# Weight conversion three steps earlier and weight splits on a three-step rhythm, in a fused attention and two-layer feed-forward kernel

## The chip, the cores and the metric

The kernel runs on one core of a Trainium2 chip. The metric is the device time of one launch in microseconds. The kernel before takes 812.19 us, the median of three runs (811.95 to 813.73). PE is TensorE's matrix multiply and PEld its weight load, DVE is VectorE, ACT is ScalarE, POOL is GpSimd, and SP is the engine that issues most of the DMAs.

## The reference

```
q_pool = q.reshape(B, H, S // 2, 2, D).mean(axis=3)        # B 4, H 8, S 1152, D 64
scores = (1 / sqrt(D)) * q_pool @ k.T
attn   = softmax(scores)                                    # with 1e-9 in the denominator
x      = (attn @ v) -> heads side by side: (4, 576, 512)
xn     = (x - mean) / sqrt(var + 1e-6) * g_ln
out    = x + relu(xn @ w_ch1) @ w_ch2                       # w_ch1 512x2048, w_ch2 2048x512
```

All inputs and the output are float32.

## The kernel before, in words

**Attention.** The heads are taken in 16 pairs, four pairs for each of the four batches. A pair has nine tiles of 128 query rows against 1152 keys, so there are 16 x 9 = 144 steps, and `step(i)` (L985) writes the instructions of step i. In a step DVE reads the scores out of PSUM and finds the row maxima (`emit_max`, L410), ACT takes the exponential (L417), PE makes the scores of the next step (`emit_s`, L390 and L398) and the product with v of an earlier one (`emit_pv`).

The first 36 steps, which are batch 0, transpose the probabilities on PE (`on_pe`, L364). The steps from 36 on split each probability into a high and a low half in 16 bits. ACT makes the high half (L428). The low half is made by DVE (L437), or, in every third step (`low_on_pool`: i % 9 in 2, 5, 8), by POOL with L239 and L435. It is written one step later, in `emit_lo(i - 1)`, which also issues the transposing DMA on SP (L440). Every product with v is made two steps after its scores in batch 0 and four steps after them from then on.

**Feed-forward layer.** It is cut into units, 24 products of 256 columns (L631) or 12 or 8 products of 512 columns (L663). From step 38 on each step takes one unit from a queue (`some_units`, L962), and after the last step the rest of the queue runs alone on PE. A unit may start only when `w_done` counts enough split blocks of its part of the weights. Units with first number 0 to 3 need part 0 to 3. A unit that isn't ready leaves its step without one. The result of a second-layer unit is added to x on DVE (L677), that of a first-layer unit is written by ACT (L644) and DVE (L645).

**Weights.** The two matrices come as 32 pieces of 512 KB. `w_load(m)` issues the DMA of piece m on SP (L734), in step m. `w_bias(m)` runs on ACT (L739), in step m + 3. `w_conv(m)` puts three instructions on DVE (all seen as L105, the line of `later`) in step m + 4. Eight pieces make one of four parts, 0 to 3. When the last piece of a part is converted, `w_reduce` (L765 to L773, on DVE) and `all_max` find a scale, and `w_scales` calls `w_splits`. Seven buffers hold pieces that wait (`w_place`). Each part has four blocks, and `w_split_a`, `w_split_b` and `w_split_c` split a block into two 16-bit halves on POOL (L239 twice, then L806).

**The order of the work** is written by hand in tables. `at(i, ...)` puts a call at the end of step i, `pre(i, ...)` at its start. The splits of parts 0 and 1 go to the deque `calm`, one per step up to step 34 and two per step from 35 on. Up to step 34 each has a `gate` ahead of it (L241): a small memset on DVE (L244) that a copy on POOL (L245) waits for, so that POOL's next instructions start when DVE has come to that place. The splits of parts 2 and 3 are put in steps 40 to 58, `a`, `b` and `c` of a block in three steps that follow each other, with no gate. Each engine runs its instructions in the order in which they were written, and so does each DMA queue.

**Other names.** `warm(n)` (L1071) runs n products of the identity with itself on PE, whose result isn't used: 84 of them run while the first inputs are loaded. `load` and `load_q` fetch k, v and q of a pair. `bound` (L182, on ACT) finds the largest absolute value of an input. `take_v` (L247) brings v of the next pair into 16-bit halves on POOL, `dup_q` (L166) and `pool_q` (L162) prepare q. The buffers for k and v hold one pair each, so k of pair p + 1 is loaded when the transposes of pair p have been read.

## Time and profile before

| | before |
|---|---|
| median of 3 runs | 812.19 us |
| profiled execution, its own time | 812.42 us |
| its span in the trace | 810.6 us |
| busy: PE, PEld, DVE, ACT, POOL | 96%, 68%, 74%, 67%, 43% of the span |
| the chain that ended last, by engine | PE 65%, DVE 18%, ACT 6%, issue 4%, DMA 3%, POOL 2%, SP's queue 2% |
| step 0 to step 35 (batch 0), by the starts of L410 | 13.65 to 173.28 us |
| step 36 to step 143 | 173.28 to 689 us |
| PE alone with the rest of the units | 689 to 810.6 us |

The profiled execution is 0.23 us above the median of the runs. Its span begins with the first instruction on the core, and 1.8 us of the device time lie around it. A time "at 226.59" is counted from the span's start. A row of the timeline gives the start, the duration, the engine, the line, what is written from what, and in brackets the idle time of that engine just before, with what ended it.

### The profile page before, as it was taken

The page shows a single profiled execution, that of the slowest core. Times are in us where ns is not written, and L with a number is a line of the kernel's source. Part 1 is how long each engine was busy: PE and PEld are TensorE (multiplying, and loading weights), DVE is VectorE, ACT ScalarE, POOL GpSimd, SP SyncE. Part 2 cuts the span into 40 slices and gives each one's busy share as a digit, 9 for nine tenths or more (in the row PEclk, how much of TensorE's full clock was granted, in tenths as well). Part 3 has the DMA queues.
Part 4 walks back from the last instruction along what each step waited for, and adds up shares of the span by engine and source line. Part 5 has one row for each costly group of instructions (what it writes and reads, how often), then busy time and mean ns, then how long its engine had stood idle before and what let it go on. Part 6 is the DMA issues. An engine that isn't in the chain of part 4 may idle for free.

```text
span 810.6 us, 21296 instructions
## 1 busy us (share of the span) xinstructions
PE 782.1 (96%) x8948; PEld 552.8 (68%) x8948; DVE 596.5 (74%) x1175; ACT 545.5 (67%) x789; POOL 346.2 (43%) x338
## 2 busy tenths in 40 slices
PE   8999999989999999989999999999999999999997
PEld 6788888767565656657666666767575757766764
DVE  4699999998898787898777778888786867521121
ACT  4898989876777778787777787777687676211010
POOL 2010243489999953565442535527161533200000
PEclk9999999999999999999999999999999999999999
DMA  8736556216899989897979898987989686401001
GB/s 225 190 121 235 172 155 191 62 63 118 150 177 155 198 148 212 160 211 127 212 135 219 143 215 140 195 159 145 210 131 194 131 147 120 85 1 27 14 1 27
DMA packets 276017, 115.95 MB, mean 143 GB/s; under 512 B 259280, under 2 KB 259280, under 8 KB 275920
## 3 DMA queue, kind: packets, MB, share of 16 engines
q1 hardware_dynamic: 275440, 113.63, 68.6%
q8 instruction: 70, 1.15, 0.6%
q10 hardware_dynamic: 480, 0.95, 0.4%
q14 instruction: 27, 0.22, 0.1%
HBM read 46.14 MB, written 4.72 MB: 63 GB/s over the span
## 4 chain that ended last, share of the span: by engine, by line
PE 65%; DVE 18%; ACT 6%; issue 4%; DMA 3%; POOL 2%; SPq 2%; ACTq 0%; DVEq 0%; POOLq 0%
PE psum L663 19%; PE psum L631 18%; PE psum L390 7%; PE psum L480 7%; PE psum L471 5%; DVE pe L410 5%; DVE hl L437 3%; PE psum L447 3%; DMA vr<-in_v_dram 2%; PE psum L398 2%; ACT pe L417 1%; PE psum L321 1%; SPq L440 1%; DVE kt L271 1%; DVE ht L645 1%
## 5 line engine op out<-in xcount | busy, mean ns | idle before, releaser
L410 DVE CUSTOM_DVE_ANT_0 pe<-psum,nought,sc 128x1152 f32<-128x1152 f32 x144 | 203.1, 1410 | 29.7 <-PE psum L197 12.8
L417 ACT ACTIVATE pe<-pe,nb 128x1152 f32<-128x1152 f32 x144 | 180.3, 1252 | 32.4 <-DVE nb L410 30.9
L663 PE MATMUL psum<-wsl,ht 128*128 128x512 f16 x864 | 196.6, 379 | 2.7 <-DVE ht L645 2.1
L631 PEld LDWEIGHTS <-wsl 128*128 128x128 f16 x1920 | 169.6, 98 | 26.1 <-issue 8.5
L631 PE MATMUL psum<-xn,wsl 128*128 128x256 f16 x1536 | 176.3, 273 | 7.5 <-DVE xb L677 3.8
L663 PEld LDWEIGHTS <-ht 128*128 128x128 f16 x864 | 81.2, 98 | 91.0 <-issue 3.1
L428 ACT ACTIVATE hl<-pe 128x1152 f16<-128x1152 f32 x108 | 125.6, 1163 | 3.4
L390 PE MATMUL psum<-kt,qt 64*128 64x512 f16 (+1 forms) x960 | 119.7, 380 | 0.9 <-ACT qt L274 0.7
L644 ACT ACTIVATE ht<-psum 128x512 f16<-128x512 f32 x72 | 42.7, 593 | 113.7 <-PE psum L631 111.0
L437 DVE SCALAR_TENSOR_TENSOR hl<-pe,hl 128x1152 f16<-128x1152 f32 x72 | 113.3, 1573 | 0.0
L480 PE MATMUL psum<-vt,pt 128*128 128x65 f16 (+2 forms) x3240 | 106.8, 193 | 0.0
L645 DVE SCALAR_TENSOR_TENSOR ht<-psum,ht 128x512 f16<-128x512 f32 x72 | 49.3, 685 | 69.8 <-ACT ht L644 69.7
L480 PEld LDWEIGHTS <-pt 128*128 128x128 f16 (+1 forms) x3240 | 98.4, 100 | 2.6 <-issue 0.2
L239 POOL TENSOR_SCALAR pe<-pe 128x1152 f32<-128x1152 f32 x36 | 41.5, 1152 | 114.4 <-ACT hl L428 114.4
L435 POOL TENSOR_TENSOR hl<-pe,hl 128x1152 f16<-128x1152 f32 x36 | 85.6, 2378 | 3.0
L471 PE MATMUL psum<-pt,vt 128*65 128x128 f32 (+1 forms) x720 | 77.4, 263 | 1.2 <-DVE kt L271 1.2
L471 PEld LDWEIGHTS psum<-pt,vt 128*65 128x65 f32 x720 | 71.4, 138 | 1.6 <-DVE kt L271 1.4
L390 PEld LDWEIGHTS <-qt 64*128 64x128 f16 (+1 forms) x960 | 31.5, 96 | 47.2 <-issue 28.8
L398 PEld LDWEIGHTS <-qt 128*128 128x128 f16 (+1 forms) x320 | 17.6, 99 | 64.2 <-issue 64.0
L245 POOL COPY gate<-gate 128x1 f32<-128x1 f32 x27 | 5.0, 186 | 106.7 <-DVE gate L244 106.7
L677 DVE SCALAR_TENSOR_TENSOR xb<-psum,inv,xb 128x512 f32<-128x512 f32 x32 | 23.8, 744 | 36.3 <-PE psum L663 36.1
L453 ACT COPY pt<-psum 128x512 f32<-128x512 f32 x72 | 44.5, 637 | 8.1 <-PE psum L447 6.9
(116 smaller groups left out, 968.4 us busy)
## 6 DMA issues: line engine op xcount, KB each, us to landing
stage<-in_moe_w_ch_dram SPq DMA_DIRECT2D x32, 512.0 KB, 7.1
kr<-in_k_dram SPq DMA_DIRECT2D x16, 576.0 KB, 4.8
vr<-in_v_dram SPq DMA_DIRECT2D x16, 576.0 KB, 4.9
qr<-in_q_dram SPq DMA_DIRECT2D x31, 288.0 KB, 4.9
out_dram<-xb SPq DMA_DIRECT2D x28, 128.0 KB, 3.3
pt<-hl SPq DMA_TRANSPOSE x108, 5.6
kr<-in_k_dram SPq DMA_DIRECT2D x16, 64.0 KB, 4.2
out_dram<-xb ACTq DMA_DIRECT2D x4, 128.0 KB, 2.6
```

Of the source, the lines that this page charges most:

```text
L390: nc.tensor.matmul(out=sp[o:o + w, c0:c0 + 512], lhsT=qt[r:r + 64, qa, q0:q0 + w], rhs=kt[r:r + 64, ka, h], start=(a == 0), stop=(a == 2),)
L410: nc.vector.tensor_tensor_reduce(out=st["pe"], in0=st["s"], in1=nought[:, 0:1].to_broadcast([128, S]), scale=pair[i // C]["sc"][:, 0:1], s ...
L417: nc.scalar.activation(out=st["pe"], in_=st["pe"], func=ACTF.Exp, scale=-1.0, bias=st["nb"])
L428: nc.scalar.activation(out=hl[:, 0], in_=st["pe"], func=ACTF.Copy, scale=2.0 ** 15)
L435: nc.gpsimd.tensor_tensor(hl[:, 1], st["pe"], hl[:, 0], op=ALU.subtract)
L437: nc.vector.scalar_tensor_tensor(hl[:, 1], st["pe"], 2.0 ** 15, hl[:, 0], op0=ALU.mult, op1=ALU.subtract)
L453: nc.scalar.copy(st["pt"][:, a:b], st["s"][:, a:b])
L471: nc.tensor.matmul(out=ps[0:65, q0:q0 + w], lhsT=vt[:, h, c], rhs=pt[:, 128 * u + q0:128 * u + q0 + w], start=(u == 0), stop=(u == C - 1),)
L480: nc.tensor.matmul(out=dst[:, 0:n], lhsT=pt[:, a + u, q0:q0 + w], rhs=vt[:, h, c, x0:x0 + n], start=(u == 0 and a == 0 and n == 65), stop= ...
L631: nc.tensor.matmul(out=ps[:, o:o + n], lhsT=wsl[:, 8 * w + cc, wa, f * 128:f * 128 + 128], rhs=xn[:, xa * KD + cc, 0:n], start=(m == 0), s ...
L645: lambda: nc.vector.scalar_tensor_tensor(lo, pv, 0.0, hi, op0=ALU.max, op1=ALU.subtract),
L663: nc.tensor.matmul(out=ps, lhsT=hv[0][:, ha, f, t * 128:t * 128 + 128], rhs=wsl[:, 8 * w + 4 + f // 2, wa, (f % 2) * DM:(f % 2) * DM + DM] ...
```

## The change

Four things are changed.

- Pieces 0, 1 and 2 of the weights are loaded ahead of the steps, pieces 0 and 1 even before v of pair 0 and q of pair 1. From then on piece m is loaded in step m - 3, biased in step m (pieces 0 and 1 ahead of or in step 0, piece 2 in step 0) and converted in step m + 1. `w_reduce` moves three steps with it, and so do the splits of parts 0 and 1.
- `warm(84)` becomes `warm(72)`.
- The splits of parts 2 and 3 (eight blocks, three calls each) are put in steps 40 to 62, one block every third step: a gate with `a` and `b` in one step, a gate with `c` in the next, and no split in the third.
- In those steps the first `take_v` of a pair moves one step later (42, 51 and 60 in place of 41, 50 and 59).

```diff
+    SPLITS = 40
...
         for n in range(2):
+            u = i0 + (5, 7)[n]
             if on_pe(p * C):
-                at(i0 + (5, 7)[n], gate)
-            at(i0 + (5, 7)[n], take_v, p, n)
+                at(u, gate)
+            elif n == 0 and SPLITS <= u < SPLITS + 24:
+                u += 1
+            at(u, take_v, p, n)
...
     for m in range(32):
-        i0 = m
-        pre(i0, w_load, m)
-        at(i0 + 3, w_bias, m)
-        pre(i0 + 4, w_conv, m)
+        if m > 2:
+            pre(m - 3, w_load, m)
+        if m > 1:
+            at(m if m > 2 else 0, w_bias, m)
+        pre(m + 1, w_conv, m)
         if m % 8 == 7:
-            at(i0 + (5 if m < 16 else 4), w_reduce, m // 8)
+            at(m + (2 if m < 16 else 1), w_reduce, m // 8)
...
-            i0 = 22 + 9 * part + 5 * n // 2
-            for x, fn in ((0, w_split_a), (1, w_split_b), (2, w_split_c)):
-                at(i0 + x, fn, 4 * part + n)
+            i0 = SPLITS + 12 * (part - 2) + 3 * n
+            at(i0, gate)
+            at(i0, w_split_a, 4 * part + n)
+            at(i0, w_split_b, 4 * part + n)
+            at(i0 + 1, gate)
+            at(i0 + 1, w_split_c, 4 * part + n)
...
         load(0, "k", nc.sync)
+        w_load(0)
+        w_load(1)
+        load(0, "v", nc.sync)
         load_q(1, (nc.sync,))
-        load(0, "v", nc.sync)
+        w_load(2)
...
-        warm(84)
+        warm(72)
...
         k8_lo()
+        w_bias(0)
         emit_s(0)
         waiting.clear()
         until(q_parts[1], 7)
+        until([lambda: w_bias(1)])
         waiting.add(7)
```

**SP, the DMA queue, at the start.** `kr`, `qr` and `vr` are k, q and v, `stage` is a piece of the weights, `gsb` the gain of the layer norm. The first rows are those before, from q of pair 1 to the pieces behind v of pair 1. The second are the changed ones, behind k of pair 0.

```order
L129 DMA qr<-in_q_dram 64x1152 x2
L121 DMA vr<-in_v_dram 128x2x576
L1084 DMA gsb<-in_moe_g_ln_dram 128x4x1
L734 DMA stage<-in_moe_w_ch_dram 128x1024
L117 DMA kr<-in_k_dram 128x2x576
L118 DMA kr<-in_k_dram 128x2x64
L121 DMA vr<-in_v_dram 128x2x576
L734 DMA stage<-in_moe_w_ch_dram 128x1024 x5
```

```order
L734 DMA stage<-in_moe_w_ch_dram 128x1024 x2
L121 DMA vr<-in_v_dram 128x2x576
L129 DMA qr<-in_q_dram 64x1152 x2
L734 DMA stage<-in_moe_w_ch_dram 128x1024
L1098 DMA gsb<-in_moe_g_ln_dram 128x4x1
L734 DMA stage<-in_moe_w_ch_dram 128x1024
L117 DMA kr<-in_k_dram 128x2x576
L118 DMA kr<-in_k_dram 128x2x64
L121 DMA vr<-in_v_dram 128x2x576
L734 DMA stage<-in_moe_w_ch_dram 128x1024 x5
```

Before, one piece stood ahead of k of pair 1, and now four do.

**POOL in steps 42 to 45.** `wsl` is a block of weights that is split, `vt<-vr` and `vr<-vr` belong to `take_v`, `pe<-pe` and `hl<-pe,hl` are the low half that POOL makes. Before, from the end of step 42 to the split behind the low half in step 45:

```order
L806 TENSOR_TENSOR wsl<-wsl 128x1024
L239 TENSOR_SCALAR wsl<-wsl,gs_83 128x1024
L239 TENSOR_SCALAR vt<-vr,s 128x9x64
L239 TENSOR_SCALAR vr<-vr,s 128x576
L266 TENSOR_TENSOR vt<-vr,vt 128x9x64
L239 TENSOR_SCALAR wsl<-wsl 128x1024
L166 COPY qr<-qr 128x9x64
L806 TENSOR_TENSOR wsl<-wsl 128x1024
L239 TENSOR_SCALAR pe<-pe 128x1152
L435 TENSOR_TENSOR hl<-pe,hl 128x1152
L239 TENSOR_SCALAR wsl<-wsl,gs_83 128x1024
```

Now, from `take_v` in step 43 to the low half in step 45:

```order
L239 TENSOR_SCALAR vt<-vr,s 128x9x64
L239 TENSOR_SCALAR vr<-vr,s 128x576
L266 TENSOR_TENSOR vt<-vr,vt 128x9x64
L245 COPY gate<-gate 128x1
L239 TENSOR_SCALAR wsl<-wsl,gs_83 128x1024
L239 TENSOR_SCALAR wsl<-wsl 128x1024
L166 COPY qr<-qr 128x9x64
L245 COPY gate<-gate 128x1
L807 TENSOR_TENSOR wsl<-wsl 128x1024
L239 TENSOR_SCALAR pe<-pe 128x1152
L435 TENSOR_TENSOR hl<-pe,hl 128x1152
```

The splits stand behind gates, and none follows the low half.

**DVE in step 62**, from one row maximum (the `ISA` at L410) to the next. Before:

```order
L410 ISA pe,nb<-psum,nought,sc 128x1152
L410 ISA nb 128x1
L677 SCALAR_TENSOR_TENSOR xb<-psum,inv_90,xb 128x512
L271 SCALAR_TENSOR_TENSOR kt<-psum,s,kt 128x512
L437 SCALAR_TENSOR_TENSOR hl<-pe,hl 128x1152
```

Now, with the gates at the ends of steps 61 and 62:

```order
L244 MEMSET gate 128x1
L410 ISA pe,nb<-psum,nought,sc 128x1152
L410 ISA nb 128x1
L528 TENSOR_SCALAR r<-psum,s 128x1
L529 RECIPROCAL r<-r 128x1
L271 SCALAR_TENSOR_TENSOR kt<-psum,s,kt 128x512
L437 SCALAR_TENSOR_TENSOR hl<-pe,hl 128x1152
L244 MEMSET gate 128x1
```

The result of a second-layer unit (L677) is gone from step 62. The units that stood in steps 61 and 62 need the last block of part 3, which is now split in steps 61 and 62. They are taken from step 63 on, and every later unit moves with them: by two steps up to step 74, which had none before, and by one step from there to the end.

## Rows read from the trace of the kernel before

**Rows 1.** The page's part 1: busy time, share of the span, instructions.

```profile
PE 782.1 (96%) x8948; PEld 552.8 (68%) x8948; DVE 596.5 (74%) x1175; ACT 545.5 (67%) x789; POOL 346.2 (43%) x338
```

**Rows 2.** PE's waits, 191.03 to 232.14 us: engine, line, releaser, total, times, longest.

```profile
PE psum L631 <- DVE xb L677: 1.6, 1, 1.6
PE psum L631 <- DVE ht L645: 1.1, 2, 0.8
```

**Rows 3.** PE's waits, 232.14 to 292.7 us.

```profile
PE psum L631 <- DVE xb L677: 1.4, 1, 1.4
PE psum L631 <- DVE ht L645: 1.4, 2, 0.7
```

**Rows 4.** PE's waits, 314.36 to 357.08 us.

```profile
PE psum L631 <- DVE ht L645: 0.3, 1, 0.3
```

**Rows 5.** Timeline of steps 45 to 47.

```profile
218.18 1.40 DVE L410 CUSTOM_DVE_ANT_0 pe<-psum,nought,sc 128x1152 f32<-128x1152 f32 x1
...
219.74 2.13 POOL L806 TENSOR_TENSOR wsl<-wsl 128x1024 f16<-128x1024 f32 x1
...
221.84 1.15 POOL L239 TENSOR_SCALAR pe<-pe 128x1152 f32<-128x1152 f32 x1
...
223.07 2.38 POOL L435 TENSOR_TENSOR hl<-pe,hl 128x1152 f16<-128x1152 f32 x1
...
223.43 3.24 DVE L437 SCALAR_TENSOR_TENSOR hl<-pe,hl 128x1152 f16<-128x1152 f32 x1
...
226.59 1.40 DVE L410 CUSTOM_DVE_ANT_0 pe<-psum,nought,sc 128x1152 f32<-128x1152 f32 x1
...
229.03 1.14 PE L631 MATMUL psum<-xn,wsl 128*128 128x256 f16 x9 [1.65 <-DVE xb L677]
```

**Rows 6.** Groups on DVE, 314.36 to 357.08 us: count, busy us, mean ns, idle before.

```profile
L437 DVE SCALAR_TENSOR_TENSOR hl<-pe,hl 128x1152 f16<-128x1152 f32 x7 | 9.5, 1360 | 0.0
```

**Rows 7.** Stretches: length, busy of PE, PEld, DVE, ACT, POOL (instructions), clock, DMA share, GB/s.

```profile
7.20:9.00 1.80, 1.80 (x33) 1.80 (x32) 0.91 (x2) 1.17 (x4) 0.38 (x2) 1.00 1.00 218
9.00:13.65 4.65, 3.53 (x34) 2.38 (x33) 2.50 (x8) 1.89 (x4) 1.43 (x4) 1.00 0.88 254
```

**Rows 8.** Timeline of the start, 9 to 22 us.

```profile
9.49 0.27 PE L197 MATMUL psum<-ident,acc 128*2 128x128 f32 x1
...
14.13 0.37 SPq L117 DMA_DIRECT2D kr<-in_k_dram  x1
...
21.31 1.15 ACT L182 ACTIVATE kt<-kr 128x1152 f16<-128x1152 f32 x1
...
21.44 0.35 DVE L271 SCALAR_TENSOR_TENSOR qt<-psum,s,qt 128x128 f16<-128x128 f32 x1 [1.58 <-ACT qt L274]
```

**Rows 9.** DVE's conversions (L105) alone, steps 3 to 31: length, busy (instructions), clock, DMA.

```profile
24.83:150.76 125.93, 47.98 (x84) 1.00 0.56 170
```

**Rows 10.** Timeline of steps 33 to 35.

```profile
162.04 1.42 DVE L410 CUSTOM_DVE_ANT_0 pe<-psum,nought,sc 128x1152 f32<-128x1152 f32 x1
...
162.41 0.18 POOL L245 COPY gate<-gate 128x1 f32<-128x1 f32 x1
...
169.89 0.66 PE L321 MATMUL psum<-ident,qr 128*128 128x128 f32 x4 [1.16 <-DVE xn L593]
...
172.41 0.55 DVE L765 TENSOR_SCALAR wtop<-wtop 128x8 f32<-128x8 f32 x1
...
173.20 0.16 DVE L773 TENSOR_REDUCE wmax<-wtop 128x1 f32<-128x8 f32 x1
```

**Rows 11.** Timeline of steps 61 and 62: the two units on PE.

```profile
297.06 2.75 PE L663 MATMUL psum<-wsl,ht 128*128 128x512 f16 x12
...
302.13 1.90 PE L663 MATMUL psum<-wsl,ht 128*128 128x512 f16 x8
```

**Rows 12.** Steps 61 to 63, and steps 74 and 75, with the columns of rows 7.

```profile
292.75:306.00 13.25, 13.25 (x174) 7.41 (x173) 10.42 (x19) 10.07 (x15) 7.76 (x7) 1.00 0.96 186
352.30:361.80 9.50, 8.50 (x116) 5.97 (x116) 8.89 (x16) 7.97 (x12) 4.76 (x4) 1.00 1.06 212
```

## The prediction

> **What bounds the kernel now.** The page's busy shares come first: PE is busy for 96% of the span [rows 1], so 28.5 us of the span are PE's idle time, and a change that leaves PE's work as it is can win no more than a part of these. The question is where PE waits, and for whom. I asked for PE's waits stage by stage. From step 40 to step 47 its two largest groups are 1.6 us for L677 and 1.1 us for L645 on DVE [rows 2], and from there to step 60 they are 1.4 and 1.4 us [rows 3]. In the stretch of batch 2 without splits, 42.7 us long, only 0.3 us for L645 is left, and none for L677 [rows 4]. So DVE is late in steps 40 to 60, in the steps in which POOL splits weights.
>
> Why it is late is to be seen in steps 45 to 47 [rows 5]. DVE's low half (L437) begins at 223.43 and takes 3.24 us, where its mean is 1.36 us in the stretch without splits [rows 6]. POOL's own low half (L435) runs from 223.07 to 225.45, and L437 ends 1.2 us after that, so it waited for L435 and then ran at its usual pace. The row maximum of step 47 follows at once (226.59), and PE waits 1.65 us at 229.03 for the L677 behind it. POOL itself came to its low half late, since a split (L806, 2.13 us) stood ahead of it.
>
> **The change, part by part.** The sum is made against the profiled execution, 812.42 us, which is 0.23 us above the median of 812.19. About 0.2% (1.6 us) is what a measurement of this kernel can tell from no change.
>
> *Twelve idle products less.* The last ones ran at 33 in 1.80 us, 55 ns each [rows 7], so twelve are 0.65 us. The transposes and the product L197 that begins the first scale (at 9.49 [rows 8]) stand behind them on PE, and everything to step 0 behind that. I take -0.6. If k arrives too late to begin sooner it is -0.3.
>
> *Loads ahead.* On SP, pieces 1, 2 and 3, 1.57 MB, are now ahead of k of pair 1. At the 254 GB/s of the start [rows 7] that is 6.2 us more in the queue. Before, k was issued at 14.13 and ACT read it at 21.31 [rows 8], 7.2 us later, of which its own 0.66 MB take 2.6. So 4.6 us of the 6.2 are covered, and the queue can be moving pieces before 14.13 as well. I take +0.4, with 0 and +1.2 as the ends. ACT stands in front of L182 for that, with its copies out of PSUM and the exponential of step 2 behind it. V of pair 0 and q of pair 1 come later by up to two pieces, but POOL, which takes them, has nothing else to do there.
>
> *Conversion in steps 1 to 3.* A conversion is three DVE instructions, 47.98 us for 84, so 1.71 us [rows 9]. In step 1 DVE is idle for 1.58 us before L271 [rows 8], waiting for ACT. The 0.1 us that is over falls under ACT's work there. The bias of pieces 0 to 2 lies in ACT's gaps ahead of step 1. I take 0, at most +0.5, which the loads' upper end holds. In steps 4 to 31 each step has the same work as before, with another piece.
>
> *Steps 32 to 35.* The last three conversions leave steps 33 to 35, and `w_reduce` of part 3 moves from step 35 to step 32. It takes 0.9 us, from 172.41 to 173.36 [rows 10], and in step 32 DVE works without a pause up to the row maximum, so the exponential and PE's transposes of step 33 come 0.9 us later. In step 34 1.71 us of conversion go, and PE's wait of 1.16 us at 169.89 for L593 on DVE [rows 10] goes with them. Net -0.3. The ends are -1.2, if the reduction is hidden, and +0.9, if the wait stays.
>
> *Splits on POOL, steps 35 to 60.* POOL has four splits fewer left from batch 0, and those of parts 2 and 3 start behind a gate. The gate's copy began 0.37 us after the row maximum that followed it (162.41 against 162.04) and took 0.18 [rows 10], so `a` and `b`, or `c`, run beside L410, which takes 1.40 us beside POOL's work too (226.59 [rows 5]). What is behind the waiting gate on POOL is the low half of the next step. In step 45 it would end at 0.55 + 2.13 + 1.15 + 2.38 = 6.2 us after the row maximum, against 7.3 before (218.18 to 225.45), L437 1.2 us after that, and the row maximum of step 47 7.4 us after 218.18 in place of 8.4. That cuts 0.9 from the wait of 1.65. The wait of 1.4 us in rows 3 has the same place in the next pair of heads, so I take 1.7 for both. Of the 2.5 us for L645 [rows 2, 3] 0.7 stay, by the 0.3 in 42.7 us of rows 4, and of the other 1.8 I take two thirds, 1.2. Together -2.9. The ends are -4.8, if all but the 0.7 goes, and 0.
>
> That arithmetic lets L437 wait until POOL's instruction has ended. The Trainium skill says so as a rule: in "SBUF — State Buffer", section "Who interferes with whom", a VectorE instruction with two inputs in SBUF contends with a GpSimd instruction that reads SBUF, and the loser is blocked until the other ends. The 1.2 us after the end of L435 agree. If the two shared the port instead, L437 would be stretched by less at step 47, the 1.65 us would nearly go, and the term would be -4.2 in place of -2.9.
>
> *Two steps without a unit.* Steps 61 and 62 lose theirs, 2.75 and 1.90 us of PE [rows 11], as part 3 is done only in step 62. In steps 61 to 63 PE has no idle time in 13.25 us, DVE is busy for 10.42 and ACT for 10.07 [rows 12]. So these steps can shrink by 2.8 us at most, and 1.8 of the 4.65 is lost there. The work comes back later: step 74 had no unit, with PE idle for 1.0 us around it [rows 12], and the other unit adds its whole time at the end, where PE works alone. At best the sum is +0.8. I take +1.2, since three steps seldom run at DVE's bound, and if they don't shrink at all it is 4.65 - 1.0 = +3.65.
>
> *The sum:* -0.6 + 0.4 - 0.3 - 2.9 + 1.2 = -2.2, so 810.2 us. The gates' memsets on DVE, 16 of them, are beside the row maximum and cost nothing that I can see.
>
> **The rivals.**
>
> *All the waits go (806.6 us).* POOL has no backlog any more and DVE none to wait for: -0.6 - 1.2 - 4.8 + 0.8 and the loads hidden, -5.8. For it speaks that the stretch without splits shows next to no such waits. Against it, that the low half on POOL stays, with 2.38 us in L435.
>
> *The waits move (812.0 us).* DVE is earlier, but PE then waits for ACT or for the next bank, and only 0.7 of the 2.9 is won: -0.6 + 0.4 - 0.3 - 0.7 + 1.2 = 0. That is 812.4, and with half of the next 0.8 us won 812.0. PE's share of 96% speaks for it [rows 1]: a wait that is shortened leaves little before the next one. Against it, that rows 4 show a stretch of the same work with hardly a wait.
>
> *Held splits make POOL's low half late (815.8 us).* POOL works in order, and `c` waits for DVE while the low half stands behind it. From the step in which POOL has no backlog, the hold and `c` put the low half 0.55 + 2.13 = 2.7 us behind, with its transposing DMA, the load of the next v behind that on SP, and ACT, which waits for v. Before, steps 57 to 63 had few splits. If the 2.7 us reach ACT once, at the v loaded in step 63, and the waits of DVE stay: -0.6 + 0.4 - 0.3 + 0 + 1.2 + 2.7 = +3.4. Against it, in step 45 the low half comes earlier, by the arithmetic above.
>
> **How the numbers follow.** The forecast has 0.48, the first rival 0.12, the second 0.28, the third 0.12. The likeliest case's own range is 808.6 to 811.6. The range is 806.6 to 813.8: it holds the forecast and the second rival with the loads or the units at their upper ends, and reaches to the first. Faster by over 0.2% (under 810.6) are the first rival and 0.42 of the forecast's 0.48, 0.54. Slower (over 813.8) is the third with a little of the second, 0.13. The rest, 0.33, is the same.
>
> **What would show it.** In the changed profile the products before L285 end 0.6 us sooner. L182 on k of pair 1 waits for its DMA by no more than 1 us. L437 in steps 40 to 53 has a mean under 2.0 us, and PE's wait for L677 in step 47 is under 1 us. Steps 61 to 63 take 10.4 to 12 us, and the tail behind the last row maximum is some 2.6 us longer. The forecast is wrong if the waits for L645 and L677 keep their size, if ACT waits for k or v by 2 us or more, or if steps 61 to 63 don't get shorter.

## The result, and the profile after

The changed kernel takes 823.36 us, the median of four runs (821.32 to 824.14), against 812.88 us for the kernel before in the same comparison. The ratio is 1.0126, with a 95% interval of 1.0109 to 1.0142. It is 10.5 us slower. The forecast was 810.2 us, and its range ended at 813.8. The profiled execution took 823.51 us, with a span of 821.7 us.

First the page, its busy shares [rows 1] and the line of its part 4 that gives the chain that ended last, by engine:

```profile
PE 787.8 (96%) x8936; PEld 553.8 (67%) x8936; DVE 587.5 (71%) x1195; ACT 544.1 (66%) x789; POOL 339.4 (41%) x358
...
PE 71%; DVE 11%; POOL 8%; ACT 5%; issue 3%; DMA 1%; SPq 1%; POOLq 0%; DVEq 0%; ACTq 0%
```

PE is busy for 5.7 us longer, for 12 products less, and POOL, which had 2% of the chain before, has 8%. To see where, both executions were cut at the starts of L410. By step 40 the changed kernel is 1.1 us late; it lost 1.23 in step 0. From step 40 to step 66 it needs 5.6 us more than the 123.3 us of before (2.3 in steps 40 to 60, 3.3 in steps 61 to 65), from step 66 to the last row maximum 1.7 more, and for the tail behind that 2.6 more. These add up to the 11 us between the spans.

PE's waits, with the columns of rows 2, in steps 40 to 47 [rows 2], 48 to 60 [rows 3], and 61 to 65:

```profile
PE psum L631 <- DVE xb L677: 2.0, 1, 2.0
PE psum L631 <- DVE ht L645: 0.6, 2, 0.3
...
PE psum L631 <- DVE xb L677: 2.7, 1, 2.7
PE psum L631 <- DVE ht L645: 0.6, 2, 0.3
...
PE psum L663 <- POOL wsl L807: 2.4, 1, 2.4
PE psum L663 <- POOL wsl L239: 0.9, 1, 0.9
```

The waits for L645 have shrunk as forecast. Those for L677 have grown from 1.6 and 1.4 us, and PE waits for a split itself (L807 is `w_split_c`, which was L806 before). DVE's wait for POOL, steps 40 to 65, and the group of L437 in steps 40 to 60, first before, then now:

```profile
DVE pe L410 <- POOL hl L435: 4.5, 2, 2.3
```

```profile
L437 DVE SCALAR_TENSOR_TENSOR hl<-pe,hl 128x1152 f16<-128x1152 f32 x14 | 29.9, 2136 | 0.0
...
L437 DVE SCALAR_TENSOR_TENSOR hl<-pe,hl 128x1152 f16<-128x1152 f32 x14 | 21.5, 1537 | 0.0
```

So DVE's low half waits far less for POOL, 1.54 us in the mean and not 2.14. But the row maximum now waits twice for POOL's low half, which the kernel before shows nowhere in these steps. The timeline of steps 45 to 47 has the first of the two [rows 5]:

```profile
215.94 1.31 POOL L245 COPY gate<-gate 128x1 f32<-128x1 f32 x1
...
217.13 1.41 DVE L410 CUSTOM_DVE_ANT_0 pe<-psum,nought,sc 128x1152 f32<-128x1152 f32 x1
...
217.22 1.12 POOL L239 TENSOR_SCALAR wsl<-wsl,gs 128x1024 f32<-128x1024 f32 x1
...
220.03 0.19 POOL L245 COPY gate<-gate 128x1 f32<-128x1 f32 x1
...
220.17 2.13 POOL L807 TENSOR_TENSOR wsl<-wsl 128x1024 f16<-128x1024 f32 x1
...
222.28 1.16 POOL L239 TENSOR_SCALAR pe<-pe 128x1152 f32<-128x1152 f32 x1
...
222.81 1.84 DVE L437 SCALAR_TENSOR_TENSOR hl<-pe,hl 128x1152 f16<-128x1152 f32 x1
...
223.53 3.35 POOL L435 TENSOR_TENSOR hl<-pe,hl 128x1152 f16<-128x1152 f32 x1
...
226.91 1.42 DVE L410 CUSTOM_DVE_ANT_0 pe<-psum,nought,sc 128x1152 f32<-128x1152 f32 x1 [2.26 <-POOL hl L435]
...
229.37 1.54 PE L631 MATMUL psum<-xn,wsl 128*128 128x256 f16 x9 [2.05 <-DVE xb L677]
```

Read it from the end. PE waits for L677, which stands behind the row maximum of step 47. DVE is free at 224.65, but the row maximum begins at 226.91, when L435 has ended. The tile `pe` has three buffers (L408), so the row maximum of step 47 writes the buffer that the low half of step 44 is still read from. And L435 is late because POOL came to it late, and because L437 had begun 0.7 us before it: it took 3.35 us, against 2.38 before. No gate kept POOL waiting here: neither row of L245 has idle time before it. The last one that did, for 1.29 us, was at 203.28, and from there on POOL had no pause. It came from `take_v` at 215.94, and then `a`, `b`, the copy of q and `c` stood in a row ahead of the low half.

Step 64 has the third wait. The unit there was written behind the splits of the last block, since `w_done` counts a split when it is written, not when POOL has run it:

```profile
309.48 0.38 PE L663 MATMUL psum<-wsl,ht 128*128 128x512 f16 x1 [0.92 <-POOL wsl L239]
...
309.98 0.19 POOL L245 COPY gate<-gate 128x1 f32<-128x1 f32 x1
...
310.13 2.12 POOL L807 TENSOR_TENSOR wsl<-wsl 128x1024 f16<-128x1024 f32 x1
...
312.30 2.29 PE L663 MATMUL psum<-wsl,ht 128*128 128x512 f16 x5 [2.44 <-POOL wsl L807]
```

### The profile page after: what moved, and what is told of

The parts are those of the page before. It is cut to its first block, busy times and chain, and to the rows that moved or that the text cites. A ratio compares the mean times of both kernels' runs of the same rounds, so it can differ in the third digit from the quotient of the medians.

```text
span 821.7 us, 21307 instructions
## 1 busy us (share of the span) xinstructions
PE 787.8 (96%) x8936; PEld 553.8 (67%) x8936; DVE 587.5 (71%) x1195; ACT 544.1 (66%) x789; POOL 339.4 (41%) x358
## 4 chain that ended last, share of the span: by engine, by line
PE 71%; DVE 11%; POOL 8%; ACT 5%; issue 3%; DMA 1%; SPq 1%; POOLq 0%; DVEq 0%; ACTq 0%
PE psum L631 21%; PE psum L663 19%; PE psum L390 8%; PE psum L480 8%; PE psum L471 5%; DVE pe L410 3%; PE psum L447 3%; PE psum L398 3%; POOL hl L435 2%; POOL vt L266 1%; PE psum L321 1%; DVE hl L437 1%; ACT pe L417 1%; POOL wsl L239 1%; POOL wsl L807 1%
## 5 line engine op out<-in xcount | busy, mean ns | idle before, releaser
L410 DVE CUSTOM_DVE_ANT_0 pe<-psum,nought,sc 128x1152 f32<-128x1152 f32 x144 | 203.2, 1411 | 34.1 <-PE psum L197 14.1
L631 PE MATMUL psum<-xn,wsl 128*128 128x256 f16 x1536 | 179.6, 275 | 8.2 <-DVE xb L677 5.2
L437 DVE SCALAR_TENSOR_TENSOR hl<-pe,hl 128x1152 f16<-128x1152 f32 x72 | 104.0, 1444 | 0.0
L645 DVE SCALAR_TENSOR_TENSOR ht<-psum,ht 128x512 f16<-128x512 f32 x72 | 49.3, 685 | 75.4 <-ACT ht L644 75.4
L435 POOL TENSOR_TENSOR hl<-pe,hl 128x1152 f16<-128x1152 f32 x36 | 87.9, 2442 | 3.0
L245 POOL COPY gate<-gate 128x1 f32<-128x1 f32 x47 | 11.0, 234 | 122.8 <-DVE gate L244 122.8
L677 DVE SCALAR_TENSOR_TENSOR xb<-psum,inv,xb 128x512 f32<-128x512 f32 x32 | 23.9, 746 | 45.8 <-PE psum L663 45.6
```

The lines of the kernel that those rows point to most:

```text
L410: nc.vector.tensor_tensor_reduce(out=st["pe"], in0=st["s"], in1=nought[:, 0:1].to_broadcast([128, S]), scale=pair[i // C]["sc"][:, 0:1], s ...
L435: nc.gpsimd.tensor_tensor(hl[:, 1], st["pe"], hl[:, 0], op=ALU.subtract)
L437: nc.vector.scalar_tensor_tensor(hl[:, 1], st["pe"], 2.0 ** 15, hl[:, 0], op0=ALU.mult, op1=ALU.subtract)
L631: nc.tensor.matmul(out=ps[:, o:o + n], lhsT=wsl[:, 8 * w + cc, wa, f * 128:f * 128 + 128], rhs=xn[:, xa * KD + cc, 0:n], start=(m == 0), s ...
L645: lambda: nc.vector.scalar_tensor_tensor(lo, pv, 0.0, hi, op0=ALU.max, op1=ALU.subtract),
```

## The experiments

Theory P: a held split puts POOL's low half off, it keeps the `pe` buffer, and DVE and then PE wait. The rivals: L, the earlier loads and conversions cost; C, the shorter run of idle products disturbs TensorE's clock for the whole program; U, blocks 14 and 15 are done too late, and the units that are missing or moved cost. The granted clock is among the rivals because the changed profile shows four stretches of 3.4 us at about half clock, in step 0 and behind each of the three waits. Steps are counted by the starts of L410, and all ratios are to the kernel before, with 95% intervals. Each experiment is made from the changed kernel unless it says otherwise.

### The parts of the change, one at a time

84 products put back:

```diff
-        warm(72)
+        warm(84)
```

> The changed kernel (823.4 us), with the 84 idle products of before. Theory P (the held splits put off POOL's low half, its pe buffer and the last split, so that TensorE stands in steps 47, 56 and 64, and its clock falls behind each of these waits): only the first of the four half-clock stretches, in step 0, can go; it cost 1.23 us there against 0.56 us gained by the shorter run of products, so 822.2 to 823.4 us, with the waits of 2.05, 2.69 and 2.44 us in steps 47, 56 and 64 still there. Rival C (the shorter run of products at the start leaves the clock in a state in which it falls again later): no half-clock stretch anywhere, 812 to 816 us.

823.91 us, ratio 1.0140 (1.0123 to 1.0156), 0.5 us above P's range. The four half-clock stretches are all there, in the same places. Rival C falls, and so do the forecast's 0.6 us: with 84 products step 0 began at 12.44 us here, with 72 at 13.09.

The early conversion alone (with 84 products, and `take_v` and the splits as before):

```diff
-            i0 = SPLITS + 12 * (part - 2) + 3 * n
-            at(i0, gate)
...
+            i0 = 22 + 9 * part + 5 * n // 2
+            for x, fn in ((0, w_split_a), (1, w_split_b), (2, w_split_c)):
+                at(i0 + x, fn, 4 * part + n)
```

> The kernel before with the weights' loads, bias, conversion and reduction three steps earlier, and nothing else (84 products, the old places of the splits). Theory P: the early conversion does little: by the changed kernel's steps +1.3 us in steps 1 to 9 of which 1.23 is the half-clock stretch, -1.5 in steps 33 to 35; so 811 to 813.5 us (before: 812.9), and no wait of TensorE over 1.7 us in steps 40 to 64. Rival L (the earlier loads and conversions are what costs, through DMA queues and ACT in the first steps, and shift all that follows): 816 to 823 us.

811.40 us, ratio 0.9983 (0.9973 to 0.9993). Rival L falls: this part is a small gain.

The new places of the splits alone, in the kernel before:

```diff
-            i0 = 22 + 9 * part + 5 * n // 2
-            for x, fn in ((0, w_split_a), (1, w_split_b), (2, w_split_c)):
-                at(i0 + x, fn, 4 * part + n)
+            i0 = SPLITS + 12 * (part - 2) + 3 * n
+            at(i0, gate)
...
+                u += 1
```

> The kernel before with the new places of the second batch's splits alone (steps 40 to 62, each held behind VectorE's copy, and the value's first half a step later); loads, conversion and the 84 products as before. Theory P: nearly all of the loss, 821 to 824 us, with TensorE's waits for L677 of 2 us or more in steps 47 and 56, for the split in step 64, three half-clock stretches behind them and a tail 2.6 us longer. Rivals C and L: 812 to 815 us, of which 1.2 us or so for the units missing in steps 61 and 62.

826.25 us, ratio 1.0168 (1.0151 to 1.0185), above P's range. All of the loss is in this part. PE's waits are 2.84, 2.66 and 2.44 us in steps 47, 56 and 64. But the granted clock was full from 5.7 us until PE had finished in this profile, so one step of Theory P falls: the half-clock stretches are not needed for the loss.

72 products alone, in the kernel before:

```diff
-        warm(84)
+        warm(72)
```

> The kernel before with 72 idle products in place of 84, and nothing else. If the shorter run is what lets the clock fall in step 0 (at 14.5 us in the changed kernel): a half-clock stretch there, -0.56 and +1.23 us, so 813.2 to 813.9 us. If it is the earlier bias and conversion of weights, or the wait for k's DMA with them: no half-clock stretch, -0.6 us, 812.0 to 812.6 us. Rival C (the state of the clock carries through the program): several half-clock stretches, 816 us or more.

815.19 us, ratio 1.0029 (1.0017 to 1.0040), with no half-clock stretch in the profile. None of the three expectations fits. The profiled run was the fastest of ten (813.33), so it can't show where the others lost their time. In it, steps 66 to 75 took 1.1 us longer and steps 118 to 121 0.8 us. Why 72 products cost 2 us here, and nothing measurable in the changed kernel, stays open.

### The hold, and what stands behind it

No gates in front of the second batch's splits:

```diff
-            at(i0, gate)
...
-            at(i0 + 1, gate)
```

> The changed kernel without the gates in front of the second batch's splits, all else in its place. Theory P (c, held for VectorE, stands right ahead of POOL's low half, which keeps a pe buffer that the row maximum three steps on must write): c and the low half start up to 0.9 us sooner, TensorE's waits for L677 in steps 47 and 56 go back to the 1.65 and 1.44 us of before or less, and the last split ends some 0.7 us sooner in step 64: 819 to 822.5 us (changed kernel 823.4). Theory U (what costs is that blocks 14 and 15 are done too late: units missing in steps 61 and 62, TensorE waiting for the last split, every later unit in another step): no change by the gates, 822.5 to 824.5 us, with the wait in step 64 at 2 us or more.

818.72 us, ratio 1.0079 (1.0058 to 1.0101), 0.3 us below P's range. The waits in steps 47 and 56 are 1.50 and 0.67 us, and the row maximum never waits for L435. The gates alone cost 0.47% of the time of before, some 4 us. Against the changed kernel the profile is 4.6 us shorter in steps 40 to 60 and some 3 us in steps 61 to 65, where the last splits aren't held either.

The rhythm one step earlier, so that `c` isn't right in front of the low half:

```diff
-    SPLITS = 40
+    SPLITS = 39
```

> The changed kernel with the rhythm begun in step 39 in place of 40: c then stands in steps 40, 43, ... 61, two steps ahead of POOL's low half and not right in front of it, and each block is done one step sooner. Theory P: TensorE's waits for L677 in steps 47 and 56 are under 1.2 us, 818 to 821 us. Theory U: the waits there matter little; one missing unit and one step's delay less, 820.5 to 823 us, with waits in steps 47 and 56 of which nothing is said.

816.43 us, ratio 1.0056 (1.0035 to 1.0076), below both ranges. Steps 47 and 56 are as P expected (no wait over 0.5 us in step 47, 0.83 us in step 56). What is left is the unit that waits for the last split, now in step 63:

```profile
PE psum L663 <- POOL wsl L807: 4.8, 1, 4.8
```

Part 3 alone back in its old places:

```diff
+            if part == 3:
+                for x, fn in ((0, w_split_a), (1, w_split_b), (2, w_split_c)):
+                    at(49 + 5 * n // 2 + x, fn, 4 * part + n)
+                continue
```

> The changed kernel with part 3 alone back in its old places (steps 49 to 58, a, b and c in three steps, no gates); part 2 keeps the new rhythm. Theory U: the loss is part 3's lateness, so it goes nearly whole: tail and step 64 as before, 811 to 813 us. Theory P: the wait in step 47 stays at 2 us or more, the one in step 56 goes back to 1.4, and part 2's share of the waits stays: 813 to 816 us. If neither place matters (the loss comes from the value's first half half a step later): 820 us or more.

822.93 us, ratio 1.0130 (1.0109 to 1.0150): a miss for both theories, and in the range of the third expectation, by which the later `take_v` (the value's first half) is what costs. The tail is as before and no unit waits for a split, so Rival U's part is gone, and the time is the same. Half of its loss is in steps 40 to 65, and there in step 56, where PE waits 5.6 us. There POOL has `a`, the second half of the value, `b`, the copy of q and `c` in a row ahead of its low half, with no gate at all, and the releaser is the same:

```profile
272.27 2.36 POOL L435 TENSOR_TENSOR hl<-pe,hl 128x1152 f16<-128x1152 f32 x1
...
274.67 1.42 DVE L410 CUSTOM_DVE_ANT_0 pe<-psum,nought,sc 128x1152 f32<-128x1152 f32 x1 [3.49 <-POOL hl L435]
```

So the low half on POOL hurts whenever the work ahead of it makes it late, held or not. `take_v` is a part of that work, and no run moves it alone, so its share isn't shown. The other half of this kernel's loss, 5.4 us, lies behind step 66, 3.4 of it in steps 118 to 121, and is not explained.

All low halves of steps 41 to 62 on VectorE:

```diff
-        return i % C in (2, 5, 8)
+        return i % C in (2, 5, 8) and not 40 < i < 63
```

> The changed kernel with VectorE making all low halves of the probabilities in steps 41 to 62, seven or eight of which POOL made. Theory P: nothing stands behind a held split on POOL that the row maximum needs, so TensorE's waits for L677 in steps 47 and 56 are under 1 us; VectorE has 8 x 1.36 = 10.9 us more work in 22 steps, which it has room for (70% busy there): 817 to 821 us. Theory U: 822 to 824.5 us, since block 15 is no sooner. If VectorE has no room: 825 us or more, with waits for L645 in many steps.

813.64 us, ratio 1.0006 (0.9992 to 1.0020), below what any theory expected. With nothing behind the splits that DVE needs, the time is that of before again, though the gates, the missing units and the longer tail are all still there. Steps 40 to 65 take 5.3 us less than before the change and 10.9 less than in the changed kernel: 6.3 in steps 40 to 60, and 4.6 in steps 61 to 65, where POOL also comes to the last splits sooner (PE waits 1.2 us for them, not 3.4). So the edit takes both waits away and doesn't by itself tell Theory P from Rival U. The group of L437 in steps 40 to 60:

```profile
L437 DVE SCALAR_TENSOR_TENSOR hl<-pe,hl 128x1152 f16<-128x1152 f32 x21 | 31.0, 1478 | 0.1
```

21 low halves cost DVE 31.0 us, where 14 took 21.5 in the changed kernel: 9.5 us more. DVE is busy for 88.4 of the 97.7 us there, so it has room for them. (In the kernel before, 14 took 29.9.)

### Is the rhythm good without POOL's low half?

The same edit in the kernel before, and nothing else:

> The kernel before with VectorE making all low halves of the probabilities in steps 41 to 62, and nothing else. Theory P': POOL's low half among the splits is what makes TensorE wait in steps 45 to 60 of the kernel before too (1.65 and 1.44 us for L677, and the waits for L645), and VectorE pays little for seven more low halves, since it then waits less for the port (in the changed kernel with this edit 21 took 31.0 us, where 14 took 29.9 before): 808 to 810 us (before 812.2). Rival R (the edit only repairs what the held splits spoil): 811.5 to 813.5 us.

812.53 us, ratio 0.9997 (0.9987 to 1.0007): Rival R. In steps 40 to 60 the splits, which stand in their old places there, still get in the way of L437:

```profile
L437 DVE SCALAR_TENSOR_TENSOR hl<-pe,hl 128x1152 f16<-128x1152 f32 x21 | 39.3, 1872 | 0.1
```

That is 9.4 us more than the 29.9 of 14 in the kernel before. So the seven more cost DVE about as much here as in the changed kernel, and the expectation's premise, that VectorE pays little, was wrong: it had set two different kernels against each other.

The profile shows steps 40 to 65 2.1 us shorter, but by step 40 this execution had lost 3.0 us, with half-clock stretches at 14.4 and 178.2 us. Why the median of the others shows no gain either is open.

The early conversion and this edit, with the old places of the splits:

> The kernel before with the early conversion alone (84 products, old places of the splits, 1.4 us faster in its own run) and all low halves on VectorE in steps 41 to 62. Theory P': both gains stand beside each other, 806.5 to 809 us. Rival R: 810.5 to 812 us, the gain of the early conversion alone.

809.87 us, ratio 0.9967 (0.9955 to 0.9980), between the two ranges. This is the kernel to hold the 813.64 us above against. With all low halves on VectorE the rest of the change (the new places and the 12 products less) costs 3.8 us, with POOL's it costs 12.0 (823.36 against 811.40). So about a third of the loss stays when POOL makes no low half there. In steps 40 to 60 alone the new places of the splits lose 4.0 us with POOL's low halves (+2.3 against -1.8 us) and win 3.0 without them (-4.0 against -1.1).

The changed kernel with this edit and the rhythm from step 39:

> The changed kernel with all low halves on VectorE in steps 41 to 62 and the rhythm begun in step 39. If units that are missing or moved cost their 2.6 us in the tail and little else (813.6 us with the rhythm from 40): the tail is as before and the last splits are done a step sooner, 809 to 812 us. If TensorE's wait for the last split only moves one step ahead (4.83 us in step 63 of the run from 39 with POOL's low halves): 813 to 816 us.

811.33 us, ratio 0.9978 (0.9965 to 0.9992), in the range of the first expectation: the tail is back to 126.7 us, and the wait for the last split is 1.1 us.

The changed kernel with this edit and no gates:

> The changed kernel with all low halves on VectorE in steps 41 to 62 and no gates in front of the second batch's splits. Theory P (a gate costs by what stands behind it on POOL): with no low half on POOL the hold is nearly free, so taking the gates away wins under 1.5 us, 812 to 814 us, where it won 4.7 us with the low halves on POOL. Rival G (the hold costs by itself, through the splits that end later): 808 to 811 us.

815.86 us, ratio 1.0039 (1.0023 to 1.0056), slower than with the gates (1.0006), against both expectations. So the hold in front of the splits is worth 2 to 3 us as long as nothing that DVE needs stands behind it on POOL, and costs some 4 us if something does. In the profile the gain is in steps 40 to 60, 2.1 us, where L437 has a mean of 1478 ns with the gates and 1657 without. In steps 61 to 65 the gates cost 1.2. The profiled execution was the fastest of five, so it doesn't show the whole difference.

### Which gate

The gate in front of `c` taken away:

```diff
-            at(i0 + 1, gate)
```

> The changed kernel (823.4 us) without the gate in front of c; a and b stay held. Theory P, in its sharper form (the gate on c does it, as POOL's low half stands right behind c): the row maximum no longer waits for L435 in steps 47 and 56, and the gain of taking all gates away (818.7 us) is nearly all here: 817.5 to 820 us. If the gate on a and b does it: 822 us or more.

The gate in front of `a` and `b` taken away:

```diff
-            at(i0, gate)
```

> The changed kernel without the gates in front of a and b; c stays held. Theory P, sharper form: the row maximum still waits for L435 by some 2 us in steps 47 and 56, 821.5 to 824 us. If the gate on a and b does it: 817.5 to 820 us.

Without `c`'s gate 817.72 us, ratio 1.0065 (1.0043 to 1.0088), as P expected. Without the other one 825.08 us, ratio 1.0142 (1.0122 to 1.0163), 1.1 us above its range. Of the two gates it is the one on `c` that costs. Without it steps 40 to 60 are 3.3 us shorter, and steps 61 to 65 3.7, where the last `c` isn't held. DVE's wait in the run without the gate on `a` and `b`, then in that without `c`'s:

```profile
DVE pe L410 <- POOL hl L435: 4.5, 2, 2.3
```

```profile
DVE pe L410 <- POOL hl L435: 2.3, 1, 2.3
```

One of the two waits, in step 47, outlives `c`'s gate, which P did not expect. The rows of steps 45 to 47 above show that no gate kept POOL waiting there: `a`, `b` and `c` stand ahead of that low half, held or not. How the gate works in the other one is to be seen in steps 50 to 56, first of the changed kernel:

```profile
244.01 1.05 POOL L239 TENSOR_SCALAR wsl<-wsl 128x1024 f16<-128x1024 f32 x1
...
248.39 0.18 POOL L245 COPY gate<-gate 128x1 f32<-128x1 f32 x1 [3.33 <-DVE gate L244]
...
248.53 2.13 POOL L807 TENSOR_TENSOR wsl<-wsl 128x1024 f16<-128x1024 f32 x1
...
250.63 1.15 POOL L239 TENSOR_SCALAR pe<-pe 128x1152 f32<-128x1152 f32 x1
...
251.86 2.37 POOL L435 TENSOR_TENSOR hl<-pe,hl 128x1152 f16<-128x1152 f32 x1
...
268.19 1.53 DVE L437 SCALAR_TENSOR_TENSOR hl<-pe,hl 128x1152 f16<-128x1152 f32 x1
...
268.61 3.36 POOL L435 TENSOR_TENSOR hl<-pe,hl 128x1152 f16<-128x1152 f32 x1
...
272.00 1.42 DVE L410 CUSTOM_DVE_ANT_0 pe<-psum,nought,sc 128x1152 f32<-128x1152 f32 x1 [2.26 <-POOL hl L435]
```

Then of the kernel without `c`'s gate:

```profile
241.43 1.05 POOL L239 TENSOR_SCALAR wsl<-wsl 128x1024 f16<-128x1024 f32 x1
...
242.56 2.13 POOL L807 TENSOR_TENSOR wsl<-wsl 128x1024 f16<-128x1024 f32 x1
...
246.62 1.16 POOL L239 TENSOR_SCALAR pe<-pe 128x1152 f32<-128x1152 f32 x1 [1.94 <-ACT hl L428]
...
247.86 2.38 POOL L435 TENSOR_TENSOR hl<-pe,hl 128x1152 f16<-128x1152 f32 x1
...
264.55 2.37 POOL L435 TENSOR_TENSOR hl<-pe,hl 128x1152 f16<-128x1152 f32 x1
...
266.20 1.94 DVE L437 SCALAR_TENSOR_TENSOR hl<-pe,hl 128x1152 f16<-128x1152 f32 x1
...
268.07 1.41 DVE L410 CUSTOM_DVE_ANT_0 pe<-psum,nought,sc 128x1152 f32<-128x1152 f32 x1
```

Held, POOL stands idle for 3.33 us and then does `c` when it should already be at the low half. From `b` to the end of that low half it takes 10.2 us; free, `c` fills the time in which POOL would wait for ACT anyway, and it takes 8.8. In the steps that follow POOL has the two halves of the value and another block to do and doesn't catch up. So the next L435 comes 0.4 us behind L437 and not 1.65 us ahead of it, and ends 2.25 us behind the end of L437, where the row maximum could have started.

One gate, with `a`, `b` and `c` together behind the low half, from step 39:

```diff
-            i0 = SPLITS + 12 * (part - 2) + 3 * n
...
             at(i0, w_split_b, 4 * part + n)
-            at(i0 + 1, gate)
-            at(i0 + 1, w_split_c, 4 * part + n)
+            at(i0, w_split_c, 4 * part + n)
```

> The changed kernel with one gate and all of a, b and c in one step, every third step from 39 on, which puts them behind POOL's low half and not ahead of it; each block is done two steps sooner. Theory P: no wait of the row maximum for L435, TensorE's waits for L677 in steps 47 and 56 under 1 us, no unit missing, tail as before: 810 to 814 us. If a hold costs wherever it stands: 818 us or more.

818.93 us, ratio 1.0068 (1.0051 to 1.0084): the time is in the range of the second expectation, that a hold costs wherever it stands. The row maximum never waits for L435, as the first expected, and steps 40 to 60 are 0.8 us shorter than before (1.8 in the early conversion alone, so up to 1.0 us can be the hold's). But L677 is still waited for (1.09 us in step 56), and a unit was again written right behind the splits of the last block, which makes steps 61 to 65 3.9 us longer:

```profile
PE psum L663 <- POOL wsl L239: 1.9, 1, 1.9
PE psum L663 <- POOL wsl L807: 1.8, 1, 1.8
```

The last one puts the findings together: low halves on VectorE, 84 products, the rhythm from 39, and part 3's blocks 2.5 steps apart, so that all splits are done in step 59:

```diff
-            i0 = SPLITS + 12 * (part - 2) + 3 * n
+            i0 = SPLITS + 12 * (part - 2) + (3 * n if part == 2 else 5 * n // 2)
```

> The changed kernel with 84 products, all low halves on VectorE in steps 41 to 62, the rhythm from 39 on and part 3's blocks 2.5 steps apart, so that all splits are done in step 59 and no unit is missing. If the held rhythm is good as long as no low half stands behind it on POOL, and the moved units are what cost the rest: 807 to 809.5 us, faster than the best so far (809.9 us, early conversion with low halves on VectorE and the old places of the splits). If the denser blocks run into take_v on POOL: 810 to 813 us.

808.19 us (807.60 to 808.85), ratio 0.9936 (0.9923 to 0.9948). This is in the range of the first expectation, and faster than both kernels and than all others here.

The stretches that tell these kernels apart, in us against the kernel before, from the profiled executions:

| | steps 40 to 60 | 61 to 65 | 96 to 109 | 118 to 121 | tail |
|---|---|---|---|---|---|
| before | 101.7 | 21.6 | 65.4 | 21.0 | 126.7 |
| changed | +2.3 | +3.3 | +1.6 | +1.7 | +2.6 |
| early conversion alone | -1.8 | 0.0 | 0.0 | +0.1 | 0.0 |
| new places alone | +2.9 | +2.2 | +1.6 | +2.5 | +2.6 |
| no gates | -2.3 | +0.3 | +1.6 | +4.3 | +2.6 |
| no gate on `c` | -1.0 | -0.4 | +1.6 | +1.4 | +2.6 |
| no gate on `a`, `b` | +1.4 | +2.1 | +1.6 | +2.4 | +2.6 |
| rhythm from 39 | -3.4 | +4.5 | 0.0 | +2.3 | 0.0 |
| part 3 in its old places | +5.5 | 0.0 | 0.0 | +3.4 | 0.0 |
| `a`, `b`, `c` behind the low half | -0.8 | +3.9 | 0.0 | +3.2 | 0.0 |
| before, low halves on VectorE | +0.3 | -2.4 | 0.0 | +0.3 | 0.0 |
| early conversion, low halves on VectorE | -1.1 | -2.4 | 0.0 | +0.4 | 0.0 |
| changed, low halves on VectorE | -4.0 | -1.3 | +1.6 | +2.6 | +2.6 |
| changed, low halves on VectorE, from 39 | -3.7 | -1.5 | 0.0 | +3.4 | 0.0 |
| changed, low halves on VectorE, no gates | -2.0 | -2.5 | +1.6 | +2.1 | +2.6 |
| changed, low halves on VectorE, from 39, part 3 denser, 84 products | -3.3 | -1.6 | 0.0 | +0.4 | 0.0 |

Where two units are missing, the later ones stand in other steps, which costs 1.6 us in steps 96 to 109 and 2.6 in the tail, against 1.0 won in steps 122 to 142. The column of steps 118 to 121 isn't settled: ACT waits there for k of a later pair, whose load took 4.8 us in the kernel before and 7.1 in the kernel from 39. Its four largest values, 3.2 us and more, are those of the four profiles whose granted clock fell to half for 3.4 us in step 120.

So the changed kernel is late in two ways. Between its span and that of the early conversion alone there are 12.7 us. 4.0 of them are in steps 40 to 60, where POOL's low half is late. 3.3 are in steps 61 to 65, where a unit waits for the last splits, and 2.6 in the tail. By step 40 it is 1.0, and 1.7 from step 66 to the last row maximum.

## Why the prediction was wrong, point by point

*Idle products, -0.6.* Step 0 did begin 0.56 us sooner. But in the kernels with 84 products it began between 12.44 and 13.65 us, so this isn't theirs, and putting them back changed nothing that can be measured. Taken out of the kernel before, alone, they made it slower (815.19 us), which is not explained.

*Loads ahead, +0.4, and conversion in steps 1 to 3, 0.* L182 on k of pair 1 began at 22.02 us, 0.71 later, about the 1.23 us of step 0 less the 0.56. So the loads cost nothing. The early conversion alone changes nothing in steps 1 to 8.

*Steps 32 to 35, -0.3.* Steps 33 to 35 took 1.5 us less, and not where I said. The wait of 1.16 us for L593 [rows 10] stayed, with 1.12, and step 34 took only 0.1 us less. Steps 33 and 35 took 0.7 us less each, and step 32, which now has the reduction, was not longer. PE's wait of 0.78 us ahead of the scores in step 33 went down to 0.31.

*Splits on POOL, -2.9.* This is the step that failed first. It was the arithmetic for step 45: POOL's low half would end 6.2 us after the row maximum, as `c` begins 0.55 us behind it. `c` began 3.04 us behind it (220.17 against 217.13), since `a`, `b` and the copy of q were still to do, and L435 took 3.35 us and not 2.38, since L437 was now ahead of it. That makes 9.75 us, later than the 7.3 of before. Both gates had opened without making POOL wait. I had taken for granted that POOL is idle when the gate opens, and looked only for DVE waiting on POOL's port, not for what the low half keeps in the meantime. The term is wrong in sign: the new places cost 4.0 us in steps 40 to 60 (+2.3 against the -1.8 of the early conversion alone). The 3.0 us that they win there with the low halves on VectorE are close to the 2.9 of the sum, but that is another kernel, without the low half that the sum got wrong. L437's mean, which was to show the step right (under 2.0 us), came out at 1.60 in steps 40 to 53, while the time was lost. The measure was met, and it was the wrong one. Two slips change nothing: 8.4 less 7.4 is 1.0 and not 0.9, and the stretch of rows 4 and 6 is steps 66 to 74, mostly in batch 1.

*That L437 waits till POOL's instruction has ended.* It holds, in both directions. In step 46 L437 ended at 224.65, and from there to the end of L435 it is 2.23 us, against the 2.37 us that L435 takes undisturbed. The Trainium skill, "SBUF — State Buffer", section "Who interferes with whom", adds that the order of issue, not the kind of operation, decides who blocks. The two fences on steps 50 to 56 agree: with the same pair of instructions L435 takes 3.36 us when it is second and 2.37 when it is first.

*Two steps without a unit, +1.2.* Steps 61 to 63 took 12.01 us, the upper end of what was to be seen, and the tail 2.6 us more, as forecast. With the columns of rows 7, against the 13.25 us of [rows 12]:

```profile
296.14:308.15 12.01, 10.00 (x157) 6.05 (x156) 10.17 (x22) 9.32 (x14) 11.57 (x11) 1.00 0.84 152
```

I counted the missing units alone. Not in the sum were the unit in step 64 that waits 3.4 us for the last splits, and the moved units of steps 96 to 109. This is the second step that failed, by its size: 3.3 us in steps 61 to 65, 0.7 in steps 72 to 75, 1.6 in steps 96 to 109, -1.0 in steps 122 to 142 and 2.6 in the tail make 7.2 and not 1.2. About 1 us of it is a half-clock stretch in step 64: the new places alone have 2.2 in steps 61 to 65, without one.

*The rivals.* "Held splits make POOL's low half late" was nearest, with 0.12, and it is right for one part of the loss. Its place was wrong (the load of v, ACT, step 63). The late low half reaches PE through the three `pe` buffers, twice, and only one of the two goes with the gate on `c`. The other part, the wait for the last splits, was in no rival.

## What to carry to other kernels

Before an instruction is held or moved on an engine that works in order, list what stands behind it there and, for each tile that this reads or writes, which buffer it keeps from whom: with three buffers a consumer that is late by a step stops the producer three steps on. A wait that shrinks proves nothing until the one that releases the next instruction has been looked at. And work that is counted ready when it is written, not when it has run, needs a step's distance from its user.

## What the runs showed of the hardware

TensorE's granted clock fell behind some waits and not behind others. The columns are those of rows 7. The changed kernel in step 47 and behind it:

```profile
225.00:229.60 4.60, 2.55 (x41) 1.46 (x40) 2.65 (x6) 2.54 (x4) 4.16 (x4) 1.00 0.42 84
229.60:233.00 3.40, 3.40 (x20) 2.50 (x18) 2.62 (x6) 1.40 (x3) 2.33 (x3) 0.55 1.01 206
```

The kernel with the new places alone, at the same time:

```profile
225.00:229.60 4.60, 1.76 (x37) 1.56 (x36) 3.04 (x6) 2.72 (x4) 3.77 (x4) 1.00 0.47 87
229.60:233.00 3.40, 3.40 (x46) 2.39 (x45) 2.24 (x6) 1.04 (x2) 2.71 (x3) 1.00 0.98 212
```

PE was busy for 2.55 of 4.60 us, and then the clock was at 0.55, near the lower of its two levels (1.2 GHz); in the other kernel it was busy for 1.76 us and kept the upper level (2.4 GHz). What decides this is open. The half-clock stretch cost the changed kernel PE time behind the wait, 20 products in 3.4 us where the other made 46, but over steps 40 to 65 the two kernels lost about the same, 5.6 and 5.1 us. In step 0 such a stretch appears in seven of the eighteen profiles, with 72 products and with 84, and costs 1.2 to 1.6 us in that step. So of two single profiles a difference of that size in the first steps can't be put down to the edit.
